# Queries of the last batch turned by the DMA crossbar, key pieces spread out, last output rows in two column parts

## The chip, the cores and the metric

One core of a Trainium2 chip runs the whole program. The metric is device microseconds of one execution, the median of several. Runs of this kernel fall in two groups, 0.8 us apart for the kernel before, told by the mean granted clock of TensorE that each run lists (0.954 to 0.958, or 0.961 to 0.965); one run of before (242.74 us at 0.965) doesn't fit. Where that matters, I compare within a group. A ratio is the mean time of one kernel's fast runs over the mean time of the other kernel's fast runs of the same rounds, so it is not quite the ratio of the medians that I quote.

PE is TensorE's matmul row in the profile, DVE is VectorE, ACT ScalarE, POOL GpSimd, SP SyncE. PSUM is the memory that TensorE writes its products to; a product is "emptied" or "cast" when another engine copies it out. A bubble is a stretch in which PE stands still.

## The reference, cut to what matters

```
P = sort_net; five times: row softmax, then columns normalised           # 8 x 8 per head
k_sorted, v_sorted = P applied to the 8 key and value blocks of each head
scores = scale * q_block @ k_sorted_block.T ; attn = softmax(scores) @ v_sorted
x   = attention output, tokens x 512                                      # 4 batches x 768 tokens
out = (s * relu(x @ w_in)**2 + b) @ w_out                                 # 512 -> 2048 -> 512
```

There are 8 heads of 64 columns. The kernel cuts the 3072 tokens into eight tiles of 384, two for each batch.

## The kernel before

In the second FFN product (`ffn2`) every fourth matmul is followed by a slot; a queue puts a piece of the attention of later tiles there. `S2` is two score pieces with their exponentials, `P2` two products with the values and their normalisation, `K` a key piece, `q_piece` a query piece (24 transposes on PE and one evacuation), `T` the transpose of a finished tile by the DMA crossbar. All pieces but `T` take PSUM from the pool `psa`, which has three buffers. In the profiles, `hps` is the first FFN product and `ops` the second, `ot` its output rows; `tk` and `ks` are a key piece before and after its casts, `tq` and `qt` the same for queries, `sc` the scores, `pv` the product with the values, `rec` and `x` its normalisation, `xt` the turned tile.

```
def load_q(b, part=slice(0, 128)):                  # long runs: 6 tokens of one head, 1536 B
    nc.gpsimd.dma_start(out=qr[b][part].rearrange("p h t d -> p h (t d)"),
        in_=q[b].rearrange("h (p t) d -> p h (t d)", t=TQ)[part])

def q_piece(b, hp0, eng):
    ps = psa.tile([128, 2, 1024], BF, tag="a", name="tq")
    for i in range(2):
        for t in range(TQ):
            for e in range(2):
                nc.tensor.transpose(out=ps[...], in_=qr[b][:, 2 * (hp0 + i) + e, t, :], identity=ident)
    evac(QT[b][...], ps[...], eng)                   # eng "v": VectorE, "s": ScalarE

def ffn2(t, slot=nothing):
    gt = GT.pop(t)
    for m in range(TG // 128):
        ops = psb.tile([128, d_model], FP, tag="b", name="ops")
        for f in range(NF):                          # NF = 16 matmuls of 512 columns
            nc.tensor.matmul(out=ops, lhsT=gt[...], rhs=wo_at(f), ...)
            if f % 4 == 3:
                if f == NF - 1: ...                  # flush: ot = ops * s + bias on VectorE, store on SP
                slot()
# ... the stage that the change edits
at4, at5 = attn(4), attn(5)                          # [S2, nothing, P2, S2, nothing, P2, nothing, T]
for i, n in enumerate((1, 4, 6)):
    at4[n] = K(3, 32 * i, 16, "vsv"[i])
at5[1] = lambda: q_piece(3, 0, "s")
at5[4] = lambda: q_piece(3, 2, "v")
qu = Queue(at4 + at5, 24)                            # 16 entries over 24 slots
ffn2(2, qu)
ffn2(3, qu)
```

The softmax here doesn't subtract the row's maximum and nothing guards it: scores larger than these inputs give would overflow.

## Time and profile before

| | before |
|---|---|
| time, median of 3 runs | 241.98 us (241.63 to 242.0) |
| PE busy | 227.1 of 241.1 us, 94% |
| edited stage (ffn2 of tiles 2 and 3), first ops matmul to first hps matmul of tile 4 | 119.38 to 149.61, 30.23 us |
| last matmul to the end | 237.19 to 241.1, 3.9 us |

How to read it: with PE at 94% only PE's own instructions and PE's standstills can be won. The prediction shows those lines. The columns are start, length, and the link of the chain.

```profile
136.92 0.49 PE sc L358 x16
137.41 0.97 PE ops L468 x4
138.38 0.79 PE tq L259 x24
...
141.00 0.54 PE pv L385 x16
141.53 0.86 PE ops L468 x4
```

Four ops matmuls take 0.86 us behind a pv piece and 0.97 behind a score, key or query piece.

### The profile page before, as it was taken

What the parts mean: (1) busy time and instruction counts of PE and PEld (TensorE: products, weight loads), DVE (VectorE), ACT (ScalarE), POOL (GpSimd) and SP (SyncE); (2) the same over time, 40 slices, a digit from 0 to 9 for tenths busy, and PEclk for the clock granted to TensorE, in tenths of its full rate; (3) what the DMA queues carried; (4) which work ended last, traced back from release to release, by engine and by line L of the source; (5) the groups of instructions that cost most, each with busy time, mean ns of one, the idle gap of its engine ahead of it and who ended that gap; (6) DMA issues with size and microseconds to landing.
All of it is one profiled execution on the core that took longest, in us unless ns stands there. A gap on an engine that the chain in (4) does not pass through costs nothing.

```text
span 241.1 us, 4882 instructions
## 1 busy us (share of the span) xinstructions
PE 227.1 (94%) x2059; PEld 136.1 (56%) x2080; DVE 134.1 (56%) x268; ACT 107.9 (45%) x154; POOL 39.2 (16%) x52
## 2 busy tenths in 40 slices
PE   8869799989999999999998999999999999999993
PEld 4468698845545555555554455666554556654441
DVE  5775547967993558766465748343353544342221
ACT  6356456435438451677626250656522225660000
POOL 7820000099960000460000000000000000000000
PEclk9965569999999999999999999999999999999998
DMA  4999999985999993599902061400014232001212
GB/s 63 187 199 212 216 201 206 219 206 103 141 153 178 273 307 97 123 120 112 146 7 87 3 152 46 109 0 3 1 52 122 67 111 45 0 3 43 82 48 87
DMA packets 29622, 27.33 MB, mean 113 GB/s; under 512 B 16928, under 2 KB 23840, under 8 KB 29088
## 3 DMA queue, kind: packets, MB, share of 16 engines
q0 software_dynamic: 8400, 15.21, 38.0%
q1 hardware_dynamic: 21200, 11.81, 20.6%
q8 instruction: 16, 0.26, 0.5%
q14 instruction: 6, 0.05, 0.1%
HBM read 29.63 MB, written 8.65 MB: 159 GB/s over the span
## 4 chain that ended last, share of the span: by engine, by line
PE 84%; DVE 6%; DMA 6%; issue 2%; POOL 1%; ACT 1%; POOLq 0%
PE hps L442 34%; PE ops L468 34%; DMA vb<-in_v_dram 6%; PE sc L358 3%; PE pv L385 3%; PE tv L303 2%; PE tk L277 2%; PE tq L259 2%; DVE x L390 2%; PE tv L333 1%; DVE gt L447 1%; DVE vn L228 1%; DVE ot L459 1%; PE tq L244 1%; DVE ks L228 1%
## 5 line engine op out<-in xcount | busy, mean ns | idle before, releaser
L442 PE MATMUL hps<-xt,wi 128*128 128x384 bf16 (+1 forms) x576 | 89.8, 313 | 1.0 <-DVE xt L228 1.0
L468 PE MATMUL ops<-wo,gt 128*128 128x512 bf16 x363 | 87.7, 380 | 1.5 <-issue 0.5
L446 ACT ACTIVATE rt<-hps 128x768 bf16<-128x768 f32 (+1 forms) x72 | 53.2, 739 | 53.7 <-PE hps L442 52.6
L442 PEld LDWEIGHTS <-wi 128*128 128x128 bf16 x576 | 54.6, 100 | 31.3 <-issue 2.3
L447 DVE TENSOR_TENSOR gt<-rt 128x768 bf16<-128x768 bf16 (+1 forms) x72 | 42.0, 585 | 42.2 <-ACT rt L446 41.8
L468 PEld LDWEIGHTS <-gt 128*128 128x128 bf16 x384 | 35.0, 98 | 38.4 <-issue 0.6
L361 ACT ACTIVATE at<-sc 96x768 bf16<-96x768 f32 x32 | 24.3, 802 | 35.2 <-PE sc L358 35.2
L459 DVE SCALAR_TENSOR_TENSOR ot<-ops,s_bc,bias 128x512 f32<-128x512 f32 x24 | 18.0, 749 | 38.0 <-PE ops L468 37.9
L390 DVE TENSOR_TENSOR x<-pv,rec 96x512 bf16<-96x512 f32 (+1 forms) x36 | 22.6, 628 | 1.3
L228 DVE CAST ks<-tk 64x512 bf16<-64x512 f32 (+1 forms) x36 | 20.9, 579 | 4.2 <-PE tk L277 3.8
L589 POOL TENSOR_TENSOR csum<-csum,wo 128x512 f32<-128x512 f32 x14 | 17.6, 1254 | 1.0
L230 ACT CAST ks<-tk 64x256 bf16<-64x256 f32 (+1 forms) x28 | 13.7, 490 | 8.0 <-PE tk L277 7.7
L385 PEld LDWEIGHTS <-at 96*128 96x128 bf16 (+1 forms) x256 | 12.3, 105 | 4.0 <-ACT qt L230 1.0
L385 PE MATMUL pv<-vs,at 96*128 96x66 bf16 (+1 forms) x256 | 13.0, 200 | 0.8 <-DVE rec L389 0.6
L358 PEld LDWEIGHTS <-ks 64*96 64x96 bf16 x256 | 8.4, 132 | 6.8 <-issue 5.0
L389 DVE RECIPROCAL rec<-pv 96x8 f32<-96x8 f32 (+1 forms) x36 | 6.9, 192 | 9.2 <-PE pv L385 9.2
L358 PE MATMUL sc<-qt,ks 64*96 64x96 bf16 x256 | 10.8, 223 | 1.0 <-DVE x L390 1.0
L172 PE MATMUL wp<-zt 128*128 128x256 bf16 x50 | 9.1, 300 | 1.1 <-DVE warm L104 1.1
L277 PEld LDWEIGHTS <-kb 64*128 64x128 bf16 x192 | 6.7, 98 | 5.4 <-issue 5.3
L277 PE MATMUL tk<-pd,kb 64*128 64x64 bf16 x192 | 8.2, 195 | 0.9 <-DVE pd L520 0.9
L230 ACT CAST vn<-tv 128x1024 bf16<-128x1024 f32 x6 | 6.1, 1012 | 4.1 <-PE tv L333 2.3
L303 PE MATMUL tv<-pd,vb 64*128 64x64 bf16 x64 | 6.0, 272 | 1.7 <-DMA vb<-in_v_dram 1.1
(67 smaller groups left out, 101.1 us busy)
## 6 DMA issues: line engine op xcount, KB each, us to landing
out_dram<-ot SPq DMA_DIRECT2D x24, 256.0 KB, 2.2
kb<-in_k_dram POOLq DMA_DIRECT2D x4, 768.0 KB, 10.1
vb<-in_v_dram POOLq DMA_DIRECT2D x4, 768.0 KB, 18.9
qr<-in_q_dram POOLq DMA_DIRECT2D x3, 768.0 KB, 19.3
wi<-in_moe_w_in_dram POOLq DMA_DIRECT2D x2, 1024.0 KB, 18.9
wo<-in_moe_w_out_dram POOLq DMA_DIRECT2D x2, 1024.0 KB, 30.1
dv<-vn SPq DMA_DIRECT2D x6, 256.0 KB, 6.6
vs<-dv POOLq DMA_DIRECT2D x4, 384.0 KB, 11.1
```

Source lines behind the costliest of these rows:

```text
L228: nc.vector.tensor_copy(out=out, in_=in_)
L230: nc.scalar.copy(out=out, in_=in_)
L277: nc.tensor.matmul(out=ps[:, c, :], lhsT=kb[pr, c0 + 2 * c:c0 + 2 * c + 2, :].rearrange("p c d -> p (c d)"), rhs=rhs, start=True, stop=True)
L358: nc.tensor.matmul(out=sc[:, e, n * BLK:(n + 1) * BLK], lhsT=ks[pr, g0 + n, :], rhs=QT[b][pr, hp, q0:q0 + BLK], start=True, stop=True)
L361: nc.scalar.activation(out=at, in_=sc[:, :, 0:TG], func=AF.Exp, scale=scale)
L385: nc.tensor.matmul(out=pv[e][0:m, (n - n0) * VW:(n - n0 + 1) * VW], lhsT=atf[:, c0:c0 + m], rhs=VS[b][:, gi, :], start=True, stop=True)
L390: nc.vector.tensor_tensor(out=x[:, n0:n0 + nn, hp * 128:(hp + 1) * 128].rearrange("p n (e d) -> p e n d", e=2), in0=pvv[:, :, :, 0:D], in1 ...
L442: nc.tensor.matmul(out=hps[:, f, 0:nt], lhsT=wi_at(hp, f0 + f), rhs=xt_at(t, hp, n0, nn), start=(hp == 0), stop=(hp == NHP - 1))
L446: nc.scalar.activation(out=rt[:, :, 0:nt], in_=hps[:, :, 0:nt], func=AF.Relu)
L447: nc.vector.tensor_tensor(out=gt[:, f0:f0 + 2, c0:c0 + nt], in0=rt[:, :, 0:nt], in1=rt[:, :, 0:nt], op=ALU.mult)
L459: nc.vector.scalar_tensor_tensor(out=ot, in0=ops, scalar=s_bc, in1=bias, op0=ALU.mult, op1=ALU.add)
L468: nc.tensor.matmul(out=ops, lhsT=gt[:, f, m * 128:(m + 1) * 128], rhs=wo_at(f), start=(f == 0), stop=(f == NF - 1))
```

## The change

Its intent: take 48 transposes off the PE by loading the last batch's queries token-major and turning them with the crossbar; spread the key pieces of batch 3 so that none stands in the way of scores; shorten the end by letting the last vector instruction and the last store be small.

```
@@ load_q
+        if b == B - 1:
+            qr[b] = qrp.tile([128, TQ, H, D], BF, tag="qr", name=f"qr{b}")
+            for t in range(TQ):                       # six loads, runs of one token of one head: 256 B
+                nc.gpsimd.dma_start(out=qr[b][:, t],
+                    in_=q[b][:, t * 128:(t + 1) * 128, :].rearrange("h p d -> p h d"))
+            return
+    def q_turn(b):
+        QT[b] = qtp.tile([128, NHP, S], BF, tag="qt", name=f"qt{b}")
+        for t in range(TQ):
+            nc.sync.dma_start(out=QT[b][:, :, t * 128:(t + 1) * 128],
+                              in_=qr[b][:, t].rearrange("p h d -> p (h d)"), transpose=True)
+    def last_rows(t, m):                              # the last 128 rows of the kernel
+        for c0, c1, eng in ((0, 384, nc.sync), (384, d_model, nc.scalar)):
+            # ... 16 matmuls of c1 - c0 columns, scale and bias on VectorE, store from eng
@@ the stage
-    at4, at5 = attn(4), attn(5)  # ... with K "vsv" and the two query pieces
-    qu = Queue(at4 + at5, 24)
+    qu = Queue([S2(4, 0), K(3, 0, 16, "s"), nothing, P2(4, 0), nothing, S2(4, 2), nothing,
+                K(3, 32, 16, "s"), P2(4, 2), nothing, T(4), K(3, 64, 16, "v"), S2(5, 0), nothing,
+                nothing, P2(5, 0), nothing, S2(5, 2), nothing, P2(5, 2), nothing, T(5),
+                lambda: q_turn(3), nothing], 24)
```

More of the change, by code (lines that the diff above doesn't have):

```diff
@@ L78, in load_q @@
     def load_q(b, part=slice(0, 128)):
+        if b == B - 1:
+            qr[b] = qrp.tile([128, TQ, H, D], BF, tag="qr", name=f"qr{b}")
+            for t in range(TQ):
+                nc.gpsimd.dma_start(
+                    out=qr[b][:, t],
+                    in_=q[b][:, t * 128:(t + 1) * 128, :].rearrange("h p d -> p h d"))
+            return
         if b not in qr:
@@ L461, in flush @@
             nc.sync.dma_start(out=out[r0:r0 + 128, :], in_=ot)
+    def last_rows(t, m):
+        gt = GT[t]
+        r0 = t * TG + m * 128
+        for c0, c1, eng in ((0, 384, nc.sync), (384, d_model, nc.scalar)):
+            ops = psb.tile([128, d_model], FP, tag="b", name="ops")
+            for f in range(NF):
+                nc.tensor.matmul(out=ops[:, 0:c1 - c0], lhsT=gt[:, f, m * 128:(m + 1) * 128],
+                                 rhs=wo_at(f)[:, c0:c1], start=(f == 0), stop=(f == NF - 1))
+            ot = osb.tile([128, d_model], FP, tag="ot", name="ot")
+            nc.vector.scalar_tensor_tensor(out=ot[:, 0:c1 - c0], in0=ops[:, 0:c1 - c0], scalar=s_bc,
+                                           in1=bias[:, c0:c1], op0=ALU.mult, op1=ALU.add)
+            eng.dma_start(out=out[r0:r0 + 128, c0:c1], in_=ot[:, 0:c1 - c0])
     def ffn2(t, slot=nothing):
-        gt = GT.pop(t)
+        gt = GT[t]
         for m in range(TG // 128):
+            if t == NT - 1 and m == TG // 128 - 1:
+                last_rows(t, m)
+                return
             ops = psb.tile([128, d_model], FP, tag="b", name="ops")
@@ L618 @@
     load_q(3)
-    at4, at5 = attn(4), attn(5)
-    for i, n in enumerate((1, 4, 6)):
-        at4[n] = K(3, 32 * i, 16, "vsv"[i])
-    at5[1] = lambda: q_piece(3, 0, "s")
-    at5[4] = lambda: q_piece(3, 2, "v")
-    qu = Queue(at4 + at5, 24)
+    qu = Queue([S2(4, 0), K(3, 0, 16, "s"), nothing, P2(4, 0), nothing, S2(4, 2), nothing,
+                K(3, 32, 16, "s"), P2(4, 2), nothing, T(4), K(3, 64, 16, "v"), S2(5, 0), nothing,
+                nothing, P2(5, 0), nothing, S2(5, 2), nothing, P2(5, 2), nothing, T(5),
+                lambda: q_turn(3), nothing], 24)
     ffn2(2, qu)
```

## The prediction

> **What bounds the kernel now.** I read the page's busy shares first, then the slices, then the chain that ended last, and then the stage that the change edits.
>
> ```profile
> span 241.1 us, 4882 instructions
> PE 227.1 (94%) x2059; PEld 136.1 (56%) x2080; DVE 134.1 (56%) x268; ACT 107.9 (45%) x154; POOL 39.2 (16%) x52
> PEclk9965569999999999999999999999999999999998
> PE 84%; DVE 6%; DMA 6%; issue 2%; POOL 1%; ACT 1%; POOLq 0%
> ```
>
> TensorE (PE) is busy for 94% of the span at full granted clock, and 84% of the chain is its own work. So only two things can pay: instructions taken off PE, or stretches in which it stands still. The change edits the second FFN product of token tiles 2 and 3 (96 matmuls "ops", 128x512 each, with attention pieces for tiles 4 and 5 pushed in between, one attempt after every fourth matmul), which I cut at 119.4 to 149.6 us, and the last rows at the very end. I set that stage beside the next of its kind (170.4 to 195.6: the same 96 matmuls, attention of tiles 6 and 7, no key or query work). Busy us (and instruction counts) per engine:
>
> ```profile
> 119.40:149.60 30.20, 28.66 (x314) 15.55 (x320) 18.56 (x34) 10.69 (x14) 0.00 (x0) 1.00 0.22 61
> 170.40:195.60 25.20, 24.93 (x221) 12.94 (x224) 11.23 (x23) 6.83 (x9) 0.00 (x0) 1.00 0.23 68
> ```
>
> PE stands still for 1.54 us in the first and 0.27 us in the second. The chain inside the first stage says where:
>
> ```profile
> 122.56 0.58 PE tk L277 x16
> ...
> 123.21 0.66 issue
> 123.87 0.69 DVE ks L228
> ...
> 124.57 0.69 DVE ks L228
> ...
> 125.31 0.69 issue
> 126.00 0.75 DVE ot L459
> 126.75 0.12 DVE rec L389
> ...
> 126.90 0.70 DVE x L390
> ...
> 127.64 0.38 PE sc L358 x8
> ```
>
> Here the path leaves PE. The first key piece of batch 3 (tk) is emptied by VectorE (DVE) in four casts of 0.69 us; behind it in DVE's order stand an output row block (ot, 0.75) and the normalisation of the pv tiles (rec, x). The next score pieces (sc) need a PSUM buffer of the three-deep pool that tk and pv occupy. The list of waits for the stage has "PE sc L358 <- DVE x L390: 1.0": one bubble of about 1 us.
>
> The end of the kernel, from the timeline:
>
> ```profile
> 237.22 0.75 DVE L459 SCALAR_TENSOR_TENSOR ot<-ops,s_bc,bias 128x512 f32<-128x512 f32 x1 [2.70 <-PE ops L468]
> out_dram<-ot SPq DMA_DIRECT2D x24, 256.0 KB, 2.2
> ```
>
> PE ends at 237.2, DVE at 237.97, the last store takes its 2.2 us or so from issue to landing, and the span closes at 241.1: 3.9 us behind the last matmul.
>
> **What the Trainium skill says.** "TensorE: Matmul & The Clock Gate", section "Back-to-back issue gap", gives N/2.4 + 2.5 ns for one matmul of N columns at full clock, but also a sustained pace of 131 ns at N=512 and 81 ns at N=128. The trace sides with the formula: 45 "ops" matmuls in 9.89 us are 220 ns, and 128 "hps" matmuls of 384 columns in 20.80 us are 162.5 ns. For 128 columns the formula gives 56 ns, the other figure 81; no such stream with full weights stands in this trace, but the 16 "pv" matmuls (weights 96x128, 66 columns) in 0.54 us are 34 ns, so weight loads do not forbid 56. "DMA: Bandwidth & Descriptors", section "DMA Transpose (X-bar)", demands 2-byte data, an issue from SP or ACT, and one transposing stream at a time. The trace has six such transposes (xt), all on SP, 3.9 us median to landing; the new ones join the same queue. The same page, section "Specifications", says line rate needs 512 B or more per descriptor; the trace's closest case is vs<-dv, in 128 B runs, whose four loads keep the DMA engines at 1.0 to 1.2 of a busy share for about 15 us while moving only some 110 to 160 GB/s. So the new query load, in 256 B runs (128 B after the cast), will be slow for its size.
>
> **The change part by part.**
>
> *1. Query transposes of batch 3 leave PE.* Two pieces of 24 transposes go; on the chain each is "0.79 PE tq L259 x24". They sit in a PE-bound stage: **-1.58 us**. Their PSUM evacuations go too (ACT 1.44, DVE 1.76), both beside PE work, so worth nothing by themselves.
>
> *2. In their place.* (a) GpSimd's queue gets six loads of 128 KB written, each 128 x 8 = 1024 runs, 6144 in all, in place of one load of 1024 long runs. The issue costs GpSimd about 0.9 us each by the old one's row (0.91), some 5.5 us on an engine that has nothing else left. The data: two vs<-dv loads also have 2 x 48 x 64 = 6144 runs of 128 B, and the earlier pair on SP landed in 7.5 to 11 us. So about 10 us instead of perhaps 5. The engines are full from about 103 to 120 us and nearly empty from 120 to 125 (share 0.05), so I expect the load done near 125 to 128. It stands behind the vs loads on its queue and does not delay them. It is wanted at the queue's 23rd slot, near 145: hidden by over 15 us. (b) Six crossbar transposes on SP, 24 blocks of 128x128 in all, against 16 of 128x96 in one xt transpose (1.3 to 1.5 us of SP, 3.9 to landing): about 6 us of SP from 145, landed near 155. The first reader is the score piece of tile 6, at about 168: hidden. They stand behind the transpose of tile 5 and before one store, which nobody waits for.
>
> *3. The spread of the key pieces.* The list now has 24 entries for 24 slots, with gaps, and the key pieces are emptied by ACT, ACT, DVE. I walked the three rotating PSUM buffers through it, with a slot each 0.86 us plus the piece before: scores at slot 1 take A, B; keys at 2 take C (ACT free of it by about 5.3 us into the stage); pv at 4 takes A, B; scores at 6 (6.8 us) want C and A (free at 5.3 and 6.2): no wait. Keys at 8 want B (7.1 against 9.0); keys at 12, emptied by DVE until 17.2, block pv at 16 only if it comes before 17.2, and it comes at 18.1. The tightest is scores at 18 (20.4), wanting a pv buffer free at 19.8. So no bubble is left. What is to be had is best read by difference. PE work of the stage by the chain: 96 x 0.216 = 20.7, four score pairs 1.96, four pv pairs 2.15, three key pieces 1.73, two query pieces 1.58: 28.1. The stage took 30.2, so 2.1 us are lost. In the clean stage the same sum is 24.8 against 25.2: 0.4 lost, and eleven pieces instead of eight may raise that to 0.6. So the spreading gives **-1.5 us** (1.0 of it the bubble, the rest small restarts of 0.1 to 0.2). New length: 26.6 + 0.6 = 27.1, against 30.2.
>
> *4. Last rows in two parts.* Last block now: 16 matmuls of 512 columns, 3.46 us. New: 16 x 162.5 ns = 2.60, and 16 x 56 ns = 0.90: 3.50, so +0.04 (at 81 ns it would be +0.44). DVE's last instruction: 750 ns for 512 columns, and rec takes 192 for 8; by a straight line through the two (other operations, so an estimate) 128 columns are 325 ns, say 0.35, so -0.40. The first part's 0.62 us on DVE is over before the second's matmuls are. The last store carries 64 KB in place of 256: between the 1.6 us of the 8 KB load of sort_net and 2.2, so -0.3. From another queue (ACT), so it does not stand behind the first part's issue. Sum **-0.6 us**.
>
> In all -1.6 - 1.5 - 0.6 = -3.7, and 242.0 - 3.7 = 238.3; I put 238.4, as two of the terms assume that nothing new waits.
>
> **The rivals.** *A. The stage keeps its loss* (another PSUM or DVE wait takes the bubble's place; pv at slot 9 comes straight after a key piece). For it: slack of under 1 us at slot 18. Against it: DVE's load falls by 1.8 us of query copy and 2.8 us of key casts. Then only the transposes and the tail pay: 239.8. *B. The small-run query load is far slower than I reckon*, and holds SP at the 23rd slot, or drags the transpose of tile 4 (due before 146). For it: DMA share over 1.0 while vs is loading, and 6144 runs. Against it: over 15 us of slack to 145, and 20 more until tile 6's scores. If it did bite, some us: 240 to 245. *C. The tail gives nothing or costs*: 128-column matmuls at 81 ns, and a store whose fixed part is all of its 2.2 us: then 0.0 to -0.1 and a total of 238.9. *D. It pays more*: if the stage loses as little as the clean one and the tail a full 0.9, 237.7.
>
> **The range.** Between D and A: 237.3 to 239.8. Two per cent is 4.8 us, a time under 237.1: more than PE's removable work and idle time of the stage (3.1 to 3.6) and the tail can give, so 0.05. Slower by 2% needs B in a bad form: 0.02. Within 2%: 0.93.
>
> **What would show it.** Step 1: tq with 96 matmuls at that line instead of 144, PE's total down by about 1.7. Step 3: the stage from its first ops matmul to the first hps of tile 4 lasting 27.1 us, and no PE wait on DVE in it. Step 2: qt written by DMA, landed before 160, score pieces of tile 6 not waiting for it, the query load landed before 130. Step 4: last DVE instruction of 0.35 us, and 3.1 to 3.3 us from the last matmul to the end in place of 3.9. The prediction is wrong if the chain shows a DMA or SP in the middle of the kernel, if the bubble moves to another score piece, or if other stages shift.

## The result, and the profile after

The changed kernel takes 238.31 us (median of 4 runs, 237.97 to 239.34) beside 241.99 before: ratio 0.9859, 95% interval 0.9827 to 0.989. That is 3.7 us less, within 2%. A second set of runs (below) gave 0.9856.

The head of its page:

```profile
span 236.6 us, 4840 instructions
PE 223.9 (95%) x2029; PEld 134.3 (57%) x2048; DVE 129.8 (55%) x264; ACT 108.8 (46%) x157; POOL 43.7 (18%) x57
```

PE shows 3.2 us less busy time and is still the bound; part of that is the clock's (e12, the changed kernel again at a lower clock, has 224.9). The spans differ by 4.5 us and the times by 3.7, because the two profiled runs are of different clock groups (mean granted clock 0.955 and 0.964): the first ops matmul of the kernel, ahead of everything that the change edits, starts at 61.33 us in the profile of before and at 60.37 in this one. That 0.96 us isn't the change's (in e12 it is 61.65), and I compare stages, not spans.

The edited stage, and the one after it, in the same columns as in the prediction (start:end, length, then busy us of PE, PEld, DVE, ACT, POOL, clock, DMA share, GB/s):

```profile
118.40:145.70 27.30, 26.82 (x270) 14.26 (x273) 13.90 (x29) 11.47 (x17) 0.00 (x0) 1.00 0.59 80
166.50:191.70 25.20, 24.93 (x220) 12.93 (x224) 11.21 (x23) 6.83 (x9) 0.00 (x0) 1.00 0.23 69
```

The next stage is unchanged. PE's standstill in the edited stage seems to fall from 1.54 to 0.48 us, but missing records make up more than a third of the first figure and all of the second: of the 96 ops matmuls the profile of before has 89, this one 91. The five that are missing here are the five "issue" pieces of this stage's chain, 0.48 us together, which is all of the standstill. The profile of e1 (below), where this stage is as before, has all 96, and there PE stands still for 0.96 us:

```profile
118.64:148.87 30.23, 29.27 (x321) 15.56 (x320) 18.58 (x34) 10.71 (x14) 0.00 (x0) 1.00 0.23 63
```

So the change took away 0.96 us of standstill and left none. The chain stays on PE where it left it before:

```profile
120.74 0.57 PE tk L293 x16
121.31 1.83 PE ops L501 x8
123.14 0.54 PE pv L401 x16
123.68 0.06 issue
123.74 1.67 PE ops L501 x7
125.41 0.49 PE sc L374 x16
...
145.69 20.80 PE hps L458 x128
```

The stage lasts from 118.42 to 145.69, 27.27 us: 2.96 less. The end, from the timeline:

```profile
229.64 3.66 PE L486 MATMUL ops<-wo,gt 128*128 128x384 bf16 x32
232.44 0.62 DVE L489 SCALAR_TENSOR_TENSOR ot<-ops,s_bc,bias 128x384 f32<-128x384 f32 x1 [1.85 <-PE ops L486]
233.34 0.35 DVE L489 SCALAR_TENSOR_TENSOR ot<-ops,s_bc,bias 128x128 f32<-128x128 f32 x1 [0.28 <-PE ops L486]
```

PE ends at 233.32 (in the chain the last block is 229.81 plus 3.51) and the span at 236.6: 3.3 us instead of 3.9. And the new transfers do not appear on the path: the six query transposes occupy SP from 145.8 to 155.3 and land a few us later, and the scores of tile 6, at 168.2, wait for nothing. The rows of DMA issues (KB each, median us to landing) of the query load, the query transposes and the last store:

```profile
qr<-in_q_dram POOLq DMA_DIRECT2D x6, 128.0 KB, 14.7
...
qt<-qr SPq DMA_TRANSPOSE x6, 2.8
out_dram<-ot ACTq DMA_DIRECT2D x1, 64.0 KB, 1.7
```

### The profile page after: what moved, and what is told of

Read it like the earlier page. It is cut to its first block, busy times and chain, and to the rows that moved or that the text cites. A ratio compares the mean times of both kernels' runs of the same rounds, so it can differ in the third digit from the quotient of the medians.

```text
span 236.6 us, 4840 instructions
## 1 busy us (share of the span) xinstructions
PE 223.9 (95%) x2029; PEld 134.3 (57%) x2048; DVE 129.8 (55%) x264; ACT 108.8 (46%) x157; POOL 43.7 (18%) x57
## 4 chain that ended last, share of the span: by engine, by line
PE 85%; DMA 6%; DVE 5%; issue 2%; POOL 1%; ACT 1%; POOLq 0%
PE hps L458 35%; PE ops L501 33%; DMA vb<-in_v_dram 6%; PE sc L374 3%; PE pv L401 3%; PE tv L319 2%; PE tk L293 2%; PE ops L486 1%; DVE x L406 1%; PE tq L268 1%; PE tv L349 1%; DVE gt L463 1%; DVE ks L237 1%; DVE vn L237 1%; PE tq L253 1%
## 5 line engine op out<-in xcount | busy, mean ns | idle before, releaser
L458 PE MATMUL hps<-xt,wi 128*128 128x384 bf16 (+1 forms) x576 | 88.7, 310 | 1.0 <-DVE xt L237 1.0
L501 PE MATMUL ops<-wo,gt 128*128 128x512 bf16 x349 | 84.0, 379 | 1.4 <-issue 0.5
L458 PEld LDWEIGHTS <-wi 128*128 128x128 bf16 x576 | 53.8, 99 | 31.1 <-issue 2.3
L501 PEld LDWEIGHTS <-gt 128*128 128x128 bf16 x368 | 33.6, 98 | 36.8 <-issue 0.6
L475 DVE SCALAR_TENSOR_TENSOR ot<-ops,s_bc,bias 128x512 f32<-128x512 f32 x23 | 17.2, 749 | 40.4 <-PE ops L501 40.3
L239 ACT CAST ks<-tk 64x512 bf16<-64x512 f32 (+1 forms) x32 | 16.0, 501 | 7.7 <-PE tk L293 7.4
L237 DVE CAST ks<-tk 64x512 bf16<-64x512 f32 (+1 forms) x32 | 18.1, 565 | 1.3 <-PE tk L293 0.9
L401 PEld LDWEIGHTS <-at 96*128 96x128 bf16 (+1 forms) x256 | 11.9, 104 | 4.1 <-ACT qt L239 1.0
## 6 DMA issues: line engine op xcount, KB each, us to landing
vs<-dv POOLq DMA_DIRECT2D x4, 384.0 KB, 11.9
```

The costliest lines, as they stand in the source:

```text
L237: nc.vector.tensor_copy(out=out, in_=in_)
L239: nc.scalar.copy(out=out, in_=in_)
L401: nc.tensor.matmul(out=pv[e][0:m, (n - n0) * VW:(n - n0 + 1) * VW], lhsT=atf[:, c0:c0 + m], rhs=VS[b][:, gi, :], start=True, stop=True)
L458: nc.tensor.matmul(out=hps[:, f, 0:nt], lhsT=wi_at(hp, f0 + f), rhs=xt_at(t, hp, n0, nn), start=(hp == 0), stop=(hp == NHP - 1))
L501: nc.tensor.matmul(out=ops, lhsT=gt[:, f, m * 128:(m + 1) * 128], rhs=wo_at(f), start=(f == 0), stop=(f == NF - 1))
```

## The experiments

There are twelve runs, e1 to e12 (e12 is the changed kernel again); the table has those with several timed runs that the argument compares, the others (e7, e10, e11) stand in their sections. The mean times by clock group, fast runs alone (number of runs), and the length of the edited stage in each profile, by the chain from the first ops matmul to the first hps of tile 4; "before" is the 33 runs that stood beside them, "changed" the runs of the result and of its repetition:

| kernel | clock 0.953-0.959 | clock 0.960-0.966 | ratio | stage, us | last matmul to end, us |
|---|---|---|---|---|---|
| before | 242.72 (21) | 241.89 (12) | | 30.23 | 3.91 |
| changed | 239.43 (2) | 238.43 (6) | 0.9859, 0.9856 | 27.27 | 3.28 |
| e1 tail only | 242.11 (2) | 240.99 (4) | 0.9956 | 30.23 | 3.10 |
| e2 queries by DMA only | 241.03 (5) | 240.61 (1) | 0.9939 | 28.43 | 4.05 |
| e3 first key piece on ACT | 241.70 (4) | 240.47 (2) | 0.9952 | 29.07 | 3.94 |
| e4 spread, queries on PE | 241.55 (4) | 240.19 (2) | 0.9944 | 29.07 | 3.94 |
| e5 changed, no spread | 239.03 (2) | 238.52 (2) | 0.9857 | 27.27 | 3.20 |
| e8 changed, load twice | 239.07 (3) | 237.77 (1) | 0.9854 | 27.28 | 3.16 |
| e6 changed, batch 2 too | 238.81 (2) | 237.32 (1) | 0.9837 | 27.28 | 3.31 |
| e9 as e6, load held back | 237.44 (2) | 236.12 (3) | 0.9771 | 27.28 | 3.35 |

The parts e1 to e4 differ from each other by less than their intervals (about 0.003 each way), so the stage lengths, which come out of the traces and repeat to 0.01 us (before and e1; changed, e5, e8 and e12), carry the argument, and the times confirm it.

**e1: the last rows alone.** The edit: `last_rows` and its call, as in the diff, put in the kernel before.

> Only the last output block in two column parts, everything else as before. My theory (step 4 of the prediction): PE +0.04 us, the last vector instruction 0.35 instead of 0.75 us, the last store about 0.3 us shorter: 0.5 to 0.6 us less, ratio 0.9975 to 0.998, and 3.3 us instead of 3.9 us from the last matmul to the end. Rival (the fixed part of a store is all of it, 128-column matmuls are slow): 0.0 to 0.1 us, ratio 1.000.

Ratio 0.9956 (0.9926 to 0.9985). From the last matmul to the end it took 3.10 us. The four profiles with the old tail (before, e2, e3, e4) have 3.91 to 4.05 there, 3.96 on average; six with the new one (changed, e1, e5, e8, e9, e12) 3.10 to 3.35, 3.22 on average. The last block's matmuls take 3.51 us instead of 3.46. So the tail is worth 3.96 - 3.22 - 0.05 = 0.7 us, a little above what was expected, and the rival is out.

**e2: the queries by DMA alone.**

```
-    at5[1] = lambda: q_piece(3, 0, "s")
-    at5[4] = lambda: q_piece(3, 2, "v")
+    at5[7] = seq(T(5), lambda: q_turn(3))      # and load_q, q_turn as in the diff
```

> Only the query path of batch 3 by DMA (small-run load and crossbar), the key pieces where they were, nothing in the two slots of the query pieces. My theory: the transposes were on the path, so 2 x 0.79 = 1.6 us less, ratio 0.993 to 0.9935, and the bubble of about 1 us at the second score pieces of tile 4 stays. Rival (the new load or the crossbar costs something on the path): less than 0.8 us gained, with a wait on a DMA or on SP in the chain. Second rival (the spread, not the transposes, gave the gain): 0 to 0.3 us.

Ratio 0.9939 (0.9917 to 0.996); the stage lasts 119.24 to 147.67, 28.43 us: 1.80 less, not 1.58. The bubble is still there, as in this chain:

```profile
125.17 0.69 issue
125.86 0.75 DVE ot L473
...
126.75 0.70 DVE x L404
...
127.50 0.38 PE sc L372 x8
```

The extra 0.22 us are two times 0.11: each query piece also made the four ops matmuls behind it 0.11 us longer (0.97 us instead of 0.86). Why it does so, and a pv piece doesn't, no run here shows (the last section has a candidate).

**e3: one letter.**

```
-        at4[n] = K(3, 32 * i, 16, "vsv"[i])
+        at4[n] = K(3, 32 * i, 16, "ssv"[i])
```

> Before, with one letter changed: the first key piece of batch 3 is emptied by ScalarE instead of VectorE, its place in the list kept. If the 1 us bubble comes from VectorE's queue (four casts of 0.69 us ahead of the output row and the pv tiles), it goes: 0.9 to 1.1 us less, ratio 0.9955 to 0.9965. Rival (the bubble comes from the place of the piece in the three-deep PSUM rotation, and ScalarE's casts of 2.35 us plus the two exponentials before them block it as well): 0 to 0.3 us.

Ratio 0.9952 (0.9925 to 0.9979). The stage lasts 119.21 to 148.28, 29.07 us, 1.16 less, and PE has no gap left in it:

```profile
122.40 0.57 PE tk L277 x16
122.97 1.83 PE ops L468 x8
124.80 0.54 PE pv L385 x16
125.33 0.86 PE ops L468 x4
126.20 0.49 PE sc L358 x16
```

And as a window, in the columns used above:

```profile
119.20:148.30 29.10, 29.10 (x323) 15.50 (x321) 15.94 (x30) 12.92 (x18) 0.00 (x0) 1.00 0.27 70
```

So the bubble was VectorE's queue, as its chain said, and the same place of the piece in the PSUM rotation does no harm once ScalarE empties it. The stage wins 1.16 us where PE had stood still for 0.96; before, the bubble also split the score piece into two halves of 0.38 us each, which here runs whole in 0.49.

**e4: the spread, with the queries left on PE** (the list of the changed kernel, `q_piece(3, 0, "s")` in its fifteenth entry and `q_piece(3, 2, "v")` in its twenty-first).

> The spread list of the changed kernel with its engines for the key pieces, but the query pieces still on PE (in two of its empty slots), the old contiguous load, the old tail. My theory (step 3): the bubble and the small restarts go, the transposes stay: 1.3 to 1.5 us less, ratio 0.994 to 0.9945. Rival (the query pieces are what fills the PSUM rotation, so the spread alone only moves the bubble): 0 to 0.6 us less, with a wait on VectorE or ScalarE somewhere in the stage.

Ratio 0.9944 (0.9916 to 0.9972); the stage lasts 119.21 to 148.28, 29.07 us. That is e3's length to the hundredth. The gain that I had put down to spreading comes whole with the engine of the first key piece; the 24 places add nothing to it. The places with the old engine were not run: in the new list the scores come four slots behind the first key piece instead of three, so, as an estimate, four ops matmuls (0.86 us) of the 1.16 could have gone without the letter too.

**e5: the changed kernel without the spread** (the order of before with e3's letter, the queries by DMA, the new tail).

> The changed kernel without the spread: the order of before, the first key piece emptied by ScalarE (the one letter of e3), queries by DMA, the new last rows. If the spread itself does nothing beyond that letter, the stage from the first ops matmul to the first hps of tile 4 lasts 27.27 us, as in the changed kernel, and the ratio is about 0.985. If the places matter once the query pieces are gone, the stage is 0.2 us or more longer.

Ratio 0.9857 (0.9829 to 0.9886), stage 118.81 to 146.08, 27.27 us: again the changed kernel's length. With the first key piece on ScalarE, the places don't matter when the query pieces are gone either. The parts add up: 30.23 - 1.80 (e2) - 1.16 (e3) = 27.27.

**e8: the small-run load twice,** a copy into a spare tile ahead of the real one.

```
+            spare = const.tile([128, TQ, H, D], BF, name="spare")
+            for t in range(TQ):
+                nc.gpsimd.dma_start(out=spare[:, t], in_=q[b][...])     # the same six loads
```

> The changed kernel with the small-run query load done twice, the copy (to a tile that nobody reads) ahead of the real one. The real load was done at about 122 us and is wanted at about 144 us. My theory (hidden by some 20 us): the real load is done about 10 us later, near 132 us, and the time does not change (ratio to before still 0.985, stage 27.2 to 27.4 us). Rival (the load's contention reaches the path): the stage longer by 0.5 us or more, by a wait on vs, on the transpose of tile 4, or on SP.

Ratio 0.9854 (0.9826 to 0.9883), stage 27.28 us. In the changed kernel the DMA engines are busy until about 121 us, here until about 127. Windows of the two, first the changed kernel's, then this one's (the last number but one is the DMA share):

```profile
122.00:124.00 2.00, 1.94 (x24) 1.17 (x24) 0.82 (x2) 1.68 (x3) 0.00 (x0) 1.00 0.08 10
```

```profile
122.00:124.00 2.00, 2.00 (x20) 1.01 (x16) 0.00 (x0) 1.79 (x4) 0.92 (x2) 1.00 3.61 146
126.00:128.00 2.00, 2.00 (x25) 1.08 (x24) 0.42 (x1) 1.42 (x2) 0.00 (x0) 1.00 1.63 177
```

Six thousand more runs cost some 5 to 6 us of DMA time, not the 10 expected, and nothing of it reaches PE. The load is hidden with about 20 us to spare.

**e6: batch 2 by DMA as well.**

```
-        if b == B - 1:
+        if b >= B - 2:
-  ... S2(3, 2), lambda: q_piece(2, 0, "v"), P2(3, 2), T(3), lambda: q_piece(2, 2, "v")], 24)
+  ... S2(3, 2), nothing, P2(3, 2), T(3), lambda: q_turn(2)], 24)
```

> The changed kernel with the queries of batch 2 loaded in small runs and turned by the crossbar as well (two more query pieces off the PE). If a query piece is worth 0.90 us wherever the PE is the bound, 1.8 us less than the changed kernel: about 236.5 at the same clock, ratio near 0.978. If the DMA engines, full from 60 to 120 us, make it late: a wait of the first score pieces of tile 4 (at 119 us) or of its pv pieces on a DMA, and part or all of the gain gone.

Three of its six runs were slow (241.4 to 245.5 us), the fast ones 237.32, 238.01 and 239.6; ratio of the fast ones 0.9837 (0.9797 to 0.9876). The profiled run, a fast one, shows where part of the gain went, in its chain:

```profile
86.42 7.99 DMA xt<-x
94.42 0.05 issue
94.46 1.47 PE hps L458 x8
```

The crossbar transpose of tile 2 took 8.0 us to land (6.0 for the slowest such transpose of the changed kernel), and the first product of tile 2 stood 0.7 us waiting for it. The stage of ffn2 on tiles 0 and 1 (60.96 to 94.46) lasts 33.50 us against 34.49 in the changed kernel: 1.0 won instead of 1.8.

**e9: the same with the load held back.**

```
+    def late_q2():
+        gate1 = sk.tile([1, 1], BF)
+        nc.gpsimd.tensor_copy(out=gate1, in_=XT[2][0:1, 0, 0:1])     # waits for tile 2's transpose
+        load_q(2)
-  ... T(2), P2(3, 0), ...
+  ... seq(T(2), late_q2), P2(3, 0), ...        # and no load_q(2) with the key loads
```

> As e6 (queries of batch 2 by DMA too), but its small-run load is issued only when the transpose of tile 2 has landed. In e6 that transpose took 8 us to land and the PE waited 0.7 us for it. If the load in its way was the cause, the wait goes, the second query pieces give their 1.8 us in full (about 236.5 at the clock of the changed kernel's usual runs), and the slow runs of e6 are gone. If the transpose is late for another reason, or the load now comes too late for the scores at 119 us, the time stays at 237.5 or more.

Median 236.82 us over six runs, ratio 0.9771 (0.9744 to 0.9797), where the changed kernel in the same rounds gave 0.9856. It beats both kernels: 236.12 on average in the upper clock group against 238.43. In its profile the gate passed at 89.4, 4.2 us after the transpose was issued at 85.25, and no PE wait on a DMA is left in the stage; 59.80 to 92.60 is 32.80 us, 1.7 less than the changed kernel. So the load in the transpose's way was the cause of e6's wait. Held back, it stands in the way of the next transpose, that of tile 3, which took 9.7 us to land; PE did not wait for it. One of the six runs was slow (242.38 us at a clock of 0.957). No profile fell in such a run, so why this version and e6 have runs of that kind stays open.

**e7: both last stores on SP** (`nc.scalar` to `nc.sync` in `last_rows`).

> The changed kernel with both stores of the last block on SP. The first store is issued at 233.09 for 0.33 us, the second is ready at 233.7: no queueing, so 3.2 to 3.4 us from the last matmul to the end, as in the changed kernel. If a second queue was needed, 0.2 us or more longer.

A single run, profiled: from the last matmul (234.10) to the end (237.3) 3.2 us. The second queue isn't needed. "DMA: Bandwidth & Descriptors" of the Trainium skill, section "Issuing engines are not separate DMA queues", says that starting from several engines only saves the issue time; here the first issue (233.88, for 0.33 us) is over before the second store's data are ready (234.48), so there was none to save.

**e11: the last block cut 256 and 256.**

> The changed kernel with the last block cut 256 and 256. The last vector instruction should be about 0.48 us (a line between 0.35 for 128 and 0.62 for 384 columns), the last store 128 KB: from the last matmul to the end 3.4 to 3.5 us against 3.3 in the changed kernel and 3.9 before. If the cut's size does not matter, 3.3.

The last vector instruction took 0.48 us and the end came 3.47 us after the last matmul (234.33 to 237.8). That is more than in any profile with parts of 384 and 128 columns (3.10 to 3.35): 0.13 us of it is VectorE's, and the rest is no more than these profiles differ among themselves; the 32 matmuls took 3.51 us, the same as with 384 and 128.

**e12: the changed kernel again.**

> The changed kernel, unaltered, in the same rounds as e9, e10 and e11: ratio 0.984 to 0.987, runs in two groups about 1 us apart by granted clock (0.954 to 0.958 and 0.964), as the runs of before fall in two groups.

238.48, 238.68, 238.81 at a clock of 0.964 and 239.52 at 0.954; ratio 0.9856 (0.9834 to 0.9878).

**e10: fillers against the low clock at the start** (`warm_up(12)` to `warm_up(24)`, and `warm_up(8)` behind `build_pd1()`).

> The changed kernel with 20 more filler matmuls on zeros in the PE's gap before 14 us. In the changed kernel the granted clock is 0.5 from about 16 to 32 us after that gap. If the gap is what takes the clock away, the low stretch gets shorter and the mean clock rises above 0.964, with up to 2 us less; if the load from 17 us on decides it (small matmuls, waits on vb), nothing changes, or it is 0.1 to 0.5 us longer by the fillers.

It was slower than the changed kernel: ratio 0.9896 (0.9874 to 0.9918), 239.54 to 240.49 us, with the highest mean clock of all in two of its four runs (0.971; the others 0.962 and 0.964). The same windows of the changed kernel's repetition and of this one (the granted clock is the third number from the end):

```profile
16.00:18.00 2.00, 1.09 (x13) 1.12 (x14) 1.93 (x5) 1.95 (x4) 0.54 (x1) 0.50 1.18 209
...
34.00:36.00 2.00, 2.00 (x23) 1.91 (x22) 0.93 (x4) 0.92 (x2) 0.00 (x0) 0.70 1.24 207
```

```profile
16.00:18.00 2.00, 2.00 (x49) 2.00 (x45) 1.84 (x3) 1.39 (x2) 0.54 (x1) 1.00 1.21 213
...
34.00:36.00 2.00, 2.00 (x31) 1.99 (x29) 1.55 (x6) 1.11 (x3) 0.00 (x0) 0.97 1.26 212
```

The first half of the expectation came true: the stretch of low clock began at about 20 us instead of 15 and ended at about 34 instead of 35, so it was shorter. But the kernel was no faster, and the traces say why: the fillers stand ahead of the key pieces in PE's order. The first key products start at 15.46 us instead of 13.27, their casts hold the value products (PE waits 1.2 us for ScalarE), and the first hps matmul comes at 32.26 instead of 30.98. By the first ops matmul of the kernel (61.89 against 61.65) the shorter low stretch has made up most of this, and no more. A miss, which says nothing on the change.

## Why the prediction was right

The time (238.4 told, 238.31 measured) and the mechanism held, but one term was credited to the wrong part of the edit (step 3). That the total came so near is luck in part: steps 1 and 4 were told 0.2 and 0.1 us too small and step 3 0.3 too large, and these errors cancel.

- **Step 1, the transposes** (told: 1.58 us). Measured 1.80 in e2. The term left out the 0.11 us that a piece adds to the ops matmuls behind it. The step had the price of the piece alone; its sum should have been 2 x (0.79 + 0.11).
- **Step 2, the replacements are hidden.** Right. The load was done near 121 us rather than 125 to 128, the crossbar issues took 9.4 us of SP rather than 6, and neither is near the path; e8 shows the slack by doubling the load. (The pair of loads that the prediction compares with landed in 9.6 and 11.9 us, not in 7.5 to 11; 7.5 is the least of all six.)
- **Step 3, the spread** (told: 1.5 us). This step failed in its attribution: "So the spreading gives -1.5 us". The stage won 1.16 us beyond the transposes, and e3 gets all of it from the engine of the first key piece; e4 and e5 show that the places give nothing on top of that. The prediction's own reading (four casts of 0.69 us ahead in VectorE's order) pointed to the engine, and its walk through the buffers shows that there is no wait in the new list, but not that the old places needed to be left. The "small restarts of 0.1 to 0.2" that it read in the chain are gaps of missing records, as e1's chain of the same stage has none of them. What is lost besides the bubble belongs to the pieces: before, nine pieces with 0.11 us are 1.0 of the 2.1 us lost; after, seven are 0.77, and 27.27 - 26.56 = 0.71 us is what was lost. So the spread could not take these away, and the 0.6 told for what stays was near.
- **Step 4, the tail** (told: 0.6 us). Measured 0.7, as worked out under e1. The 128-column matmuls run at 57 ns: 3.51 us less 16 x 0.1625, divided by 16. The 0.35 us of VectorE is as told.
- **The rivals.** A (a new wait in the stage) and B (the load on the path) did not come in the changed kernel. B did come in e6, where the same kind of load stood in the way of a transpose with little slack. C and D miss in the tail: it gave neither nothing nor the full 0.9. The range's lower end (237.3) stands 0.4 us under D, without a reason given.

The sum of the parts by the traces is 1.80 + 1.16 + 0.7 = 3.7 us, and the medians differ by 3.7.

## What to carry to other kernels

When a change moves a piece in a list and also changes its engine, test the two apart: here one letter did what a whole new order seemed to do. Count a small piece between large matmuls with what it does to the next large ones, not by its own length alone. Work taken off the bound and given to DMA is free only where the transfers that it stands before have slack; holding such a load back until the pressing transfer has landed cost nothing in the fast runs and gave the rest of the gain. And count the records before reading a small standstill: here more than a third of it before, and all of it after, was matmuls missing from the trace.

## What the Trainium skill lacked or had wrong

- "TensorE: Matmul & The Clock Gate", section "Back-to-back issue gap": its sustained paces, 81 ns at N=128 and 131 ns at N=512, aren't seen here. With a weight load before each matmul, the runs show 57 ns (128 columns), 110 ns (256, e11: 3.51 us by 32), 162.5 (384) and 216 (512, 20.73 us by 96 in e2): the section's formula N/2.4 + 2.5, which it calls that of an isolated gap, fits all four.
- The same page, section "What's actually happening": it says that the clock is set in windows of 3413 ns that run free of the kernel's start. That agrees with the runs here: PE is granted half the clock in one stretch, which begins between 13 and 21 us and lasts (by windows of 0.2 us) 20.48 us in the nine profiles of the lower clock group, 17.07 in the four of the upper one and 13.65 in e10's, which is six, five and four such windows. What the page lacks is the consequence: one window more or less (0.8 to 1.0 us of the time) is a quarter of the effect of a change worth 1.5%, so runs have to be compared at like clock, or stages by trace.
- "TensorEngine Tiling (Array Packing)", section "Key Properties", says that a change of the tiling mode drains TensorE; neither it nor another page that I found has the price. That may be what the pieces cost here: 0.11 us on the ops matmuls behind each piece whose weights have 64 rows or columns (score 64x96, key 64x128, query 128x64), none behind weights of 96x128 (pv) or 128x128 (the value pieces tv of the stage before, with 0.86 us behind each). That the mode changes there no run shows.
- "DMA: Bandwidth & Descriptors", section "DMA Transpose (X-bar)": that section has no duration. Here SP is held 1.22 us (median) for a 128x512 transpose and 1.45 for a 96x2048 one, so it hardly follows the size; they land in 2.8 and 3.9 us (medians), and a 96x2048 one in 8.0 and 9.7 beside a small-run load (e6, e9).
- The same page, section "Specifications", has 512 B as the least for line rate, but no time for a load below it. Here 6144 runs of 256 B, cast to 128 B, take about 5 to 6 us of all the engines, in windows of 146 GB/s.
